# Fixed instruction orders, a shifted operand for frequency 256 and a mean row in one product in a fused spectral-filter and MLP kernel

## The chip, the cores and the metric

The kernel runs on one core of one Trainium2 chip. The metric is device time in microseconds (us). The kernel before takes 420.15 us, the median of three runs (419.25 to 421.0).

## The reference

One block of a network, forward and backward, in one launch. Sizes: S = 2048 rows, D = 512 channels, F = 1792 hidden units; everything is bf16 in memory.

```python
def _A_ref(x, w_r, w_i):                       # spectral filter
    X = jnp.fft.rfft2(x.astype(jnp.float32), axes=(-2, -1))
    X = X * (w_r + 1j * w_i)
    return jnp.fft.irfft2(X, s=(S, D), axes=(-2, -1)).astype(jnp.bfloat16)

def _B_ref(x, w1, b1, w2, b2):                 # MLP with squared ReLU
    h = jnp.einsum('bsd,df->bsf', x, w1) + b1
    r = jnp.where(h > 0, h, 0)
    return jnp.einsum('bsf,fd->bsd', r * r, w2) + b2

mod = (silu(c) @ w_mod).reshape(c.shape[0], 6, 1, -1)   # sa, ca, ga, sb, cb, gb
h = layernorm(x) * (1 + ca) + sa
x = x + ga * _A_ref(h, w_r, w_i)
h = layernorm(x) * (1 + cb) + sb
x = x + gb * _B_ref(h, w1, b1, w2, b2)
```

The outputs are this x and the gradients of its product with a given `grad_out` with respect to x, w_r, w_i, w1, b1, w2, b2, c and w_mod (ten arrays, `out_0` to `out_9`).

## The kernel before, in words

**Rows and tiles.** The 2048 rows are 16 tiles of 128 (`NT`), dealt so that partition p holds rows 16p to 16p+15; four tiles make one of the four blocks (`NB`) of the MLP. F is cut into 14 chunks of 128 (`NFC`).

**The transform as matrix products.** The Fourier transform over rows is split into two factors, the one over channels is made shorter by folding (sums and differences of mirrored quarters, on VectorE). The forward transform has the stages F1 (L286, L287: product `psA` with the table `TA`), F2 (L324: `psB` with `Cd`, emptied into `AE` by ScalarE in L329) and F3 (L310: `psC` with `LF`, emptied into `Xs` in L312), then a complex product with the weights on VectorE (`cmul`). The inverse goes G1 (`spec_g1`, L345: `psG` with `LG`, emptied into the array `CS`, which profile lines call `utcs`), G2 (L376: `psT` with `Cf`, emptied into `Tsb` in L379) and G3 (L387: `psY` with `TAT`). The backward pass runs the same stages on the gradient.

A row of 512 real channels has 257 frequencies, 0 to 256. G1 takes the even and the odd ones of the first 256 as two sets of 128 columns of the operand `Z`. Frequency 256 is a column of its own: for it G1 has small products of one output partition each (`psF`, L358), four of them side by side in column tiles of the array, and eight copies of one partition (L366 and L368) that put their results into `CS` after the last of them.

The shift `sa` of the first layer norm acts on frequency 0 only. It enters F2 as a row, `dcrow`, in four products with an operand of one partition (L326), each after one of the four products (L324) of its first half.

**Stages in time.** Start-up builds the tables on POOL, VectorE and ScalarE, loads x, and computes the modulation vectors (`mod_row`, L604). F1 of all 16 tiles follows. Beside it and up to the first G2/G3 run the back products (`back_products`, L714: grad_out times w2, 56 groups of four products of 512 columns, emptied into `gab` by ScalarE in L719 or VectorE in L717 by turns). Then F2/F3, G1, and the MLP by block: G2/G3 with the second layer norm, hidden products (`stage_h`, L886), the outputs and the row gradients (`stage_o`, `stage_gn`, L915). From the second block on, the normed rows are brought into transposed form by a store (L838) and a transposing DMA load (`h2T`, L842). Column sums over rows (biases and modulation gradients) are products with a vector of ones: `colsums` (L776) runs four of them, for one tile of rows, in the four column tiles of the array, and accumulates in the bank `acc`; `colsums1` (L1290) does the same into `acc1` near the end. After the last block come the backward F2/F3 with the gradients of w1 (L1144) between, backward G1, then G2/G3 with the gradients of w2 (L1232), and the end of the w_mod gradients.

**What sets the order.** When the program is built, a scheduler turns the source into one fixed order of instructions for each engine. It goes by priorities: the order in the source, moved by `tc.high_priority()`, by the class `Priority` (the back products carry `Priority(tc, LATE)`, behind everything else that is ready), and by `tc.issue_after(x)`, which holds an instruction back until x has been issued. Semaphores then enforce the data dependences. DMAs are issued by the queue of the engine that calls `dma_start`; here nearly all come from SP, the loads of the spectral weights (`load_w`) and some stores from POOL, three from ScalarE at the start (L560, L561, L569).

**Buffers.** Tile pools hand out rotating buffers; a PSUM pool `bufs=2` alternates between two banks, and a product waits until the bank's last reader is done.

## Time and profile before

| what | value |
|---|---|
| median of three runs | 420.15 us (419.25 to 421.0) |
| profiled execution, span from first to last instruction | 416.3 us |
| profiled execution's own time | the page gives its span only; the median of the runs is 3.85 us longer |
| matmuls | 2407 in the program (2387 recorded), TensorE busy 391.7 us (94%) |
| VectorE, ScalarE, POOL busy | 343.7, 277.1, 60.6 us (83, 67, 15%) |
| DMA | 101.11 MB, mean 243 GB/s |
| granted TensorE clock | 1.000 |

Busy time of TensorE counts every moment in which a matmul is in flight; matmuls overlap, so it isn't work at peak rate. In groups of instructions a line gives the source line, the engine, output and inputs with their tile shape and sizes, the number, the busy time, the mean duration in ns, and the idle time just ahead of the group with what ended it. The tile shape is the part of the array in use: `128*128` is all of it, `128*32` a column tile of 32, `128*1` a column tile with one output column in use.

### The profile page before, as it was taken

The numbers are of one execution on the slowest core, as the hardware profiler recorded it, in microseconds if no ns is written. First come the engines' busy times: TensorE is split into PE (matmuls) and PEld (weight loads), VectorE is DVE, ScalarE is ACT, GpSimd is POOL, SyncE is SP. The second block draws the span as 40 slices with busy tenths as digits, with TensorE's granted clock in tenths as the row PEclk, the third lists the DMA queues.
The fourth block names the chain that finished last, engine by engine and source line by source line (L and its number), as shares of the span: only waits on it lengthen the run. The fifth ranks groups of instructions, "written<-read, shape, count | busy, mean of one in ns | idle before, by whom it ended". The sixth has DMA issues, their size and how long they took to land. (4 is left out here: it accounts for less than half of the span.)

```text
span 416.3 us, 7175 instructions
## 1 busy us (share of the span) xinstructions
PE 391.7 (94%) x2387; PEld 197.6 (47%) x2407; DVE 343.7 (83%) x827; ACT 277.1 (67%) x495; POOL 60.6 (15%) x147
## 2 busy tenths in 40 slices
PE   2789999999899999999999999999999999999996
PEld 0345445664444444444444444445555665444444
DVE  6899868977988578988897998964999784877885
ACT  4568699868884079338924776545655567897785
POOL 7437950000000000000000000001314520000000
PEclk9999999999999999999999999999999999999999
DMA  8999899979199459949976997998999999999994
GB/s 240 232 261 298 237 213 313 323 239 240 40 331 324 126 161 276 248 128 204 288 227 194 201 291 278 291 213 245 287 280 283 350 265 227 223 269 223 239 266 143
DMA packets 143923, 101.11 MB, mean 243 GB/s; under 512 B 99049, under 2 KB 126830, under 8 KB 143630
## 3 DMA queue, kind: packets, MB, share of 16 engines
q1 hardware_dynamic: 140394, 92.96, 84.1%
q0 software_dynamic: 2784, 7.10, 5.6%
q10 hardware_dynamic: 708, 0.59, 0.5%
q8 instruction: 19, 0.31, 0.3%
q14 instruction: 18, 0.15, 0.1%
HBM read 35.44 MB, written 41.60 MB: 185 GB/s over the span
## 5 line engine op out<-in xcount | busy, mean ns | idle before, releaser
L714 PE MATMUL mm<-gT,w2T 128*128 128x512 bf16 x224 | 57.9, 382 | 4.5 <-ACT gab L719 4.2
L1144 PE MATMUL mm<-gab,h_sb 128*128 128x448 bf16 x256 | 50.9, 352 | 0.0
L1232 PE MATMUL mm<-g_sb,hn 128*128 128x512 bf16 (+1 forms) x250 | 49.6, 352 | 0.8 <-ACT gw L1234 0.4
L915 PE MATMUL og<-w1T,gab 128*128 128x512 bf16 x219 | 49.9, 379 | 0.3
L915 PE MATMUL og<-w,h 128*128 128x512 bf16 x216 | 49.1, 379 | 0.4
L886 PE MATMUL mm<-h2T,w 128*128 128x512 bf16 x164 | 40.2, 379 | 0.5 <-ACT r L888 0.3
L1232 PEld LDWEIGHTS <-hn 128*128 128x128 bf16 x256 | 24.4, 98 | 23.4 <-issue 2.0
L1144 PEld LDWEIGHTS <-h_sb 128*128 128x128 bf16 x256 | 24.6, 98 | 21.8 <-issue 0.8
L886 PEld LDWEIGHTS <-w 128*128 128x128 bf16 x224 | 21.3, 98 | 27.7 <-issue 4.9
L915 PEld LDWEIGHTS <-h 128*128 128x128 bf16 x224 | 21.7, 98 | 25.6 <-DVE h L890 0.6
L915 PEld LDWEIGHTS <-gab 128*128 128x128 bf16 x224 | 21.6, 98 | 25.5 <-DVE gab L894 1.0
L714 PEld LDWEIGHTS <-w2T 128*128 128x128 bf16 x224 | 21.2, 98 | 24.2 <-issue 7.9
L888 ACT ACTIVATE r<-mm,b1col 128x512 bf16<-128x512 f32 x41 | 27.4, 688 | 6.3 <-DVE gab L894 3.3
L294 POOL MEMSET AE<- 128x2 bf16 x4 | 0.3, 103 | 188.5 <-DMA gh_dram<-gab 188.5
L928 ACT CAST G<-og 128x512 bf16<-128x512 f32 x16 | 9.2, 580 | 22.2 <-PE og L915 22.2
L329 ACT ACTIVATE AE<-psB 128x1024 bf16<-128x1024 f32 x16 | 21.8, 1363 | 1.8 <-PE psB L324 0.9
L719 ACT CAST gab<-mm 128x512 bf16<-128x512 f32 x36 | 21.0, 593 | 2.6 <-PE mm L714 2.3
L890 DVE TENSOR_TENSOR h<-r 128x1024 bf16<-128x1024 bf16 x28 | 19.2, 686 | 2.6 <-ACT r L888 2.5
L1148 ACT CAST gw<-mm 128x448 bf16<-128x448 f32 x16 | 8.6, 537 | 18.4 <-PE mm L1144 18.4
L477 DVE SCALAR_TENSOR_TENSOR gm_junk<-wmc,onef,gmbc 128x512 bf16<-128x512 bf16 x24 | 18.0, 750 | 3.3 <-ACT gmbc L467 2.2
L894 DVE TENSOR_TENSOR gab<-r,gab 128x1024 bf16<-128x1024 bf16 x28 | 19.2, 684 | 0.0
L379 ACT ACTIVATE Tsb<-psT 128x512 bf16<-128x512 f32 x32 | 18.5, 603 | 0.6 <-ACT utcs L368 0.5
(292 smaller groups left out, 818.5 us busy)
## 6 DMA issues: line engine op xcount, KB each, us to landing
h_dram<-h SPq DMA_DIRECT2D x28, 256.0 KB, 3.2
gh_dram<-gab SPq DMA_DIRECT2D x28, 256.0 KB, 3.6
w<-in_B_w_dram SPq DMA_DIRECT2D x2, 1792.0 KB, 9.0
wmc<-in_w_mod_dram SPq DMA_DIRECT2D x12, 256.0 KB, 5.8
wz_dram<-Z SPq DMA_DIRECT2D x8, 258.0 KB, 3.8
xs_dram<-Xs SPq DMA_DIRECT2D x8, 258.0 KB, 4.0
Z<-wz_dram SPq DMA_DIRECT2D x8, 258.0 KB, 6.0
Xb<-xs_dram SPq DMA_DIRECT2D x8, 258.0 KB, 8.2
```

The lines of the kernel that those rows point to most:

```text
L329: nc.scalar.activation(dst, ps.rearrange("p r (s e f) -> p (r s) e f", s=2, e=2), AF.Copy, scale=EF_S)
L379: K["Tsb"] = nc.scalar.activation(Tsb, ps, AF.Copy, scale=EF_S).ins
L477: nc.vector.scalar_tensor_tensor(out=junk, in0=wmc[:, i, :], scalar=K["onef"], in1=gmbc, op0=ALU.mult, op1=ALU.mult, accum_out=self.gsc[:, ...
L714: nc.tensor.matmul(ps, lhsT=w2T[:, dc, fc * P:(fc + 1) * P], rhs=gT[b][:, :, dc, :], start=(dc == 0), stop=(dc == 3))
L719: nc.scalar.copy(out=gaT[b][:, fc, :], in_=ps)
L886: nc.tensor.matmul(ps, lhsT=w1[:, dc, (fc + i) * P:(fc + i + 1) * P], rhs=h2T[b][:, :, dc, :], start=(dc == 0), stop=(dc == 3))
L888: nc.scalar.activation(r[:, i, :], ps, AF.Relu, bias=b1col[:, fc + i:fc + i + 1])
L890: nc.vector.tensor_tensor(h2, r, r, op=ALU.mult)
L894: K["gh"] = nc.vector.tensor_tensor(gh, r, gh, op=ALU.mult).ins
L915: nc.tensor.matmul(ps, lhsT=lhs(fc), rhs=rhs[:, fc, :], start=(fc == 0), stop=(fc == NFC - 1))
L1144: nc.tensor.matmul(ps[:, 0:W4], lhsT=h2_sb[:, t, dc * P:(dc + 1) * P], rhs=ghn[t // 4][:, t % 4, fs], start=(t == 0), stop=(t == NT - 1))
L1232: nc.tensor.matmul(ps[:, 0:w], lhsT=hns[fc][:, t, :], rhs=g_sb[:, t, c:c + w], start=(t == 0), stop=(t == NT - 1))
```

## The change

**Order.** A dictionary `ORDER` in the source holds, for each of the five engines, a permutation of its instructions, numbered as the source emits them. `set_order`, called last, adds an edge between each instruction and the next in this list; the edge is an order only, without a semaphore. All `high_priority`, `issue_after` and `Priority` are gone from the source. `Slots` takes the place of the tile pools: as many buffers as before, but each has a fixed name, and successive tiles take them in turn.

**Frequency 256.** In G1 the even frequencies are now taken from two views of `Z`: for the first output (`y = 0`) frequencies 0, 2, ..., 254 and for the second (`y = 1`) 2, 4, ..., 256, since the second of 0 is zero and of 256 only the second is needed. This makes two pairs of products of 128 columns where one pair of 256 was; the odd frequencies keep their pair of 256. `psF`, its products and its copies are gone, and its bank lets `psG` have six buffers for four. `build_cf` adapts the table `Cf`: the second set's frequencies start at 2, and the factor of the end frequency is applied per set.

**Mean row.** `dcrow` is written with its quarters in the order of `psB`, and one product over all 512 columns starts the bank; the four products of `UT` add to it.

The orders themselves also differ: the column sums of `acc` and `acc1` come in longer groups (four tiles of rows at a time), the back products mostly in groups of four, with others between. The PE order has 84 changes of tile shape before and 40 after. At the start, ScalarE issues the load of the last part of `w_mod` (L569) after the sigmoid and the four activations of L593, and SP issues the loads of x tiles 8 to 15 ahead of the halves of the transposed w2.

```diff
+class Slots:
+    def __init__(self, tc, name, bufs, **kw):
+        self.pool = tc.alloc_tile_pool(name=name, bufs=1, **kw)
+        self.bufs, self.turn = bufs, {}
+
+    def tile(self, shape, dtype, name, bufs=None):
+        n = bufs or self.bufs
+        k = self.turn.get(name, 0)
+        self.turn[name] = k + 1
+        return self.pool.tile(shape, dtype, name=f"{name}_{k % n}s" if n > 1 else name)
...
 def build_cf(tc, K, cpool, g, dr):
-    nc.vector.tensor_scalar(efc[:, 0:1], K["pidf"], 0.0, None, op0=ALU.is_equal)
-    nc.vector.tensor_scalar(efc[:, 1:2], efc[:, 0:1], 256.0, None, op0=ALU.mult)
-    nc.vector.tensor_scalar(efc[:, 2:3], efc[:, 0:1], math.sqrt(0.5) - 1.0, 1.0, op0=ALU.mult, op1=ALU.add)
+    for i, end in enumerate((0.0, 127.0)):
+        nc.vector.tensor_scalar(efc[:, i:i + 1], K["pidf"], end, None, op0=ALU.is_equal)
+    nc.vector.tensor_scalar(efc[:, 0:2], efc[:, 0:2], math.sqrt(0.5) - 1.0, 1.0, op0=ALU.mult, op1=ALU.add)
     for i in range(4):
-        nc.vector.tensor_scalar(f4[:, i:i + 1], K["pidf"], 2.0, efc[:, 1:2] if i == 1 else float(i // 2), op0=ALU.mult, op1=ALU.add)
+        nc.vector.tensor_scalar(f4[:, i:i + 1], K["pidf"], 2.0, (0.0, 2.0, 1.0, 1.0)[i], op0=ALU.mult, op1=ALU.add)
...
-    nc.vector.tensor_scalar(Cf[:, 0:2, :], Cf[:, 0:2, :], efc[:, 2:3], None, op0=ALU.mult)
+    for i in range(2):
+        nc.vector.tensor_scalar(Cf[:, i, :], Cf[:, i, :], efc[:, i:i + 1], None, op0=ALU.mult)
...
 def spec_f23(tc, K, UT, AEs, dc, dest, elementwise, after=lambda gi: None):
...
+                if extra:
+                    nc.tensor.matmul(ps[:, hh, :], lhsT=dc[0], rhs=dc[1], start=True, stop=False)
                 for c in range(4):
-                    fs = slice(P * c, P * c + P)
                     co = (0, 3, 1, 2)[c]
-                    os = slice(P * co, P * co + P)
-                    nc.tensor.matmul(ps[:, hh, os], lhsT=UT[:, c, 2 * gi + hh, :, :], rhs=K["Cd"][:, fs], start=True, stop=not extra)
-                    if extra:
-                        nc.tensor.matmul(ps[:, hh, os], lhsT=dc[0], rhs=dc[1][:, fs], start=False, stop=True)
+                    nc.tensor.matmul(ps[:, hh, P * co:P * co + P], lhsT=UT[:, c, 2 * gi + hh, :, :], rhs=K["Cd"][:, P * c:P * c + P],
+                                     start=not extra, stop=(c == 3 if extra else True))
...
 def spec_g1(tc, K, Z, CS, after=None):
-    with tc.tile_pool(name="psG", bufs=4, space=PSUM) as psG_pool, tc.tile_pool(name="psF", bufs=1, space=PSUM) as psF_pool:
-        psF = psF_pool.tile([P, 4, P], FP32, name="psF")
+    with Slots(tc, name="psG", bufs=6, space=PSUM) as psG_pool:
...
-                for ch in range(2):
+                for y in range(2):
                     for ri in range(2):
-                        nc.tensor.matmul(ps[:, ch, :], lhsT=Z[gi][:, hh, ri, ch:256:2],
-                                         rhs=K["LG"][:, n, ri:ri + 2, :].rearrange("p y m -> p (y m)"), start=(ri == 0), stop=(ri == 1))
+                        nc.tensor.matmul(ps[:, 0, P * y:P * y + P], lhsT=Z[gi][:, hh, ri, 2 * y:256 + 2 * y:2],
+                                         rhs=K["LG"][:, n, ri + y, :], start=(ri == 0), stop=(ri == 1))
+                for ri in range(2):
+                    nc.tensor.matmul(ps[:, 1, :], lhsT=Z[gi][:, hh, ri, 1:256:2],
+                                     rhs=K["LG"][:, n, ri:ri + 2, :].rearrange("p y m -> p (y m)"), start=(ri == 0), stop=(ri == 1))
...
-            if gi % 2 == 1:
-                for ri in range(2):
-                    for n in range(2 * gi - 2, 2 * gi + 2):
-                        q = 32 * (n % 4)
-                        nc.tensor.matmul(psF[q:q + 1, n // 4, :], lhsT=Z[n // 2][:, n % 2, ri, 256:257], rhs=K["LG"][:, n, ri + 1, :],
-                                         start=(ri == 0), stop=(ri == 1), tile_position=(0, q))
...
-        for i in range(4):
-            dst = CS[0:1, :, 1, i:16:4, :].rearrange("p t m b -> p m t b")
-            src = psF[32 * i:32 * i + 1, :, :].rearrange("p m (t b) -> p m t b", b=8)
...
+ENGINES = {"PE": "PE", "ACT": "Activation", "DVE": "DVE", "POOL": "Pool", "SP": "SP"}
+ORDER = {
+    "PE": (
+        "1-9 18-19 14-15 20-21 10-13 16-17 26-29 22-23 0 24-25 122-137 30-31 138-141 34-35 142-149 36-37 32-33 150-157 38-39 "
...
+def set_order(tc):
+    mine = {}
+    for i in tc.nc.cur_bb.bb.instructions:
+        kind = type(i).__name__
+        if kind.startswith("Inst") and kind != "InstRegisterMove":
+            mine.setdefault(str(i.engine).split(".")[-1], []).append(i)
+    edge = mybir.DependencyInfo(mybir.DependencyClass.NoSync, mybir.DependencyReason.DATA)
+    for name, runs in ORDER.items():
+        todo = mine[ENGINES[name]]
+        seq = []
+        for r in runs.split():
+            a, _, z = r.partition("-")
+            seq += todo[int(a):int(z or a) + 1]
...
+        for before, after in zip(seq, seq[1:]):
+            tc.add_manual_dep(after, before.name, edge, reason="order")
...
     psd = psM.tile([1, D], FP32, name="mod_ps", bufs=1)
     for c, neg in enumerate(((), (1, 3), (1, 2), (2, 3))):
-        fs = slice(P * c, P * c + P)
+        fs, co = slice(P * c, P * c + P), (0, 3, 1, 2)[c]
...
-            nc.tensor.matmul(psd[:, fs], lhsT=sacol[:, i, k:k + 1], rhs=K["Cd"][:, fs], start=(i == 0), stop=(i == 3))
+            nc.tensor.matmul(psd[:, P * co:P * co + P], lhsT=sacol[:, i, k:k + 1], rhs=K["Cd"][:, fs], start=(i == 0), stop=(i == 3))
...
-                with tc.issue_after(K["scales"]):
-                    nc.gpsimd.dma_start(Z[gi][p0_:p0_ + n, :, i, 0:DF], rows_)
+                nc.gpsimd.dma_start(Z[gi][p0_:p0_ + n, :, i, 0:DF], rows_)
...
-        with Priority(tc, LATE):
-            for fc in range(NFC):
...
+    set_order(tc)
```

## The prediction

> **What bounds the kernel now.** I read the page from the top, then its costliest groups, the waits of TensorE, and stretches of time.
>
> ```profile
> span 416.3 us, 7175 instructions
> ...
> PE 391.7 (94%) x2387; PEld 197.6 (47%) x2407; DVE 343.7 (83%) x827; ACT 277.1 (67%) x495; POOL 60.6 (15%) x147
> ...
> PE   2789999999899999999999999999999999999996
> ...
> DMA  8999899979199459949976997998999999999994
> ```
>
> TensorE has matmuls in flight for 94% of the span and is never below 8 tenths outside the two ends. The busy time says little about how close it is to its peak, since matmuls overlap, so I took the distances between the starts of consecutive matmuls. Where nothing waits they repeat: 216 ns for 512 columns, 189 for 448, 109 for 256, 56 for 128, and a quad of column tiles costs one 216. Summed over the program this undisturbed stream is 370.3 us. The first matmul starts at 5.8 us, the last ends the stream at 412.9, the rest is a tail of 3.4. So 416.3 = 5.8 + 370.3 + 36.8 + 3.4, and the 36.8 us of excess is all that an order can win back from TensorE. Its parts: 12.2 us before 40 us of the span (half-rate TensorE, first loads); 84 changes of array shape; the rest waits.
>
> What a shape change costs is seen in this stretch of the timeline (start, duration, engine, line):
>
> ```profile
> 156.22 1.03 PE L886 MATMUL pst<-h2T,w 128*128 128x512 bf16 x4
> 157.18 0.39 PE L776 MATMUL acc<-gp,ones_q 128*32 128x512 bf16 x1
> 157.18 0.39 PE L776 MATMUL acc<-y,ones_q 128*32 128x512 bf16 x1
> 157.19 0.39 PE L776 MATMUL acc<-G,ones_q 128*32 128x512 bf16 x1
> 157.19 0.39 PE L776 MATMUL acc<-q,ones_q 128*32 128x512 bf16 x1
> 157.41 0.38 PE L776 MATMUL acc<-gp,ones_q 128*32 128x512 bf16 x1
> ...
> 157.73 0.82 PE L886 MATMUL mm<-h2T,w 128*128 128x512 bf16 x3
> ```
>
> Quad to quad is 0.23 us with no change of shape; from the last quad (157.41) to the next 128x128 matmul (157.73) it is 0.32. Over the 77 changes that can be isolated the median excess is 95 ns: 84 of them are 8.0 us.
>
> The waits of TensorE (what, for what, us in total, times, longest), and four stretches (us; PE, PEld, DVE, ACT, POOL busy; clock; DMA share; GB/s):
>
> ```profile
> PE mm L714 <- ACT gab L719: 4.2, 8, 1.0
> ...
> PE psB L324 <- ACT AE L329: 1.5, 6, 0.4
> ...
> PE psT L376 <- ACT utcs L368: 0.4, 1, 0.4
> ```
>
> ```profile
> 62.00:73.00 11.00, 10.06 (x82) 6.46 (x81) 8.56 (x16) 10.99 (x19) 0.00 (x0) 1.00 1.08 309
> ...
> 104.00:125.00 21.00, 19.41 (x108) 8.94 (x107) 19.39 (x47) 17.82 (x34) 0.00 (x0) 1.00 0.60 187
> ...
> 156.00:208.00 52.00, 51.66 (x271) 22.93 (x274) 47.01 (x98) 35.30 (x64) 0.00 (x0) 1.00 0.95 230
> ...
> 312.00:364.00 52.00, 51.42 (x358) 29.44 (x358) 40.71 (x85) 34.10 (x66) 14.04 (x24) 1.00 1.08 270
> ```
>
> From 62 to 73 us ScalarE, which empties psB, psC and the back products, is full and TensorE waits for it; from 104 to 125 VectorE and ScalarE are both near full. By the distances, with 95 ns taken off per change, TensorE loses 10.4 us to waits from 40 to 140 us (1.5, 3.4, 1.3, 3.2 and 1.0 in stretches of 20), and 6.5 us from 220 to 400. From 140 to 220 nothing is left to win but the shape changes.
>
> **What the Trainium skill says.** "TensorEngine Tiling (Array Packing)", Key Properties: a change of tiling mode "drains the TensorE"; it gives no price, and the trace gives 95 ns. "TensorE: Matmul & The Clock Gate", Back-to-back issue gap: N/2.4 + 2.5 ns for an isolated warm matmul; the trace agrees (216 at 512, 56 at 128), and disagrees with the 131 ns that the section names for a sustained stream. "Perfetto Trace Analysis", Tensor Engine Instruction: ScalarE and VectorE are strict FIFO. So an evacuation listed behind one that is not ready is late too, under the old order and the new alike; both orders are fixed when the program is built.
>
> **The change part by part.** I counted in the two programs' instruction orders.
>
> Frequency 256 by a shifted operand (build_cf, spec_g1): 64 matmuls of 128x1 tiles go; they run as 16 quads, about 55 ns each: -0.9 us. Their groups bring 16 shape changes, counted below. The main products become four of 128 columns and two of 256 in place of four of 256: the same columns in 64 more matmuls, at 2.5 ns each: +0.2. The 64 extra weight loads hide under the matmuls (PEld 47%). Eight one-partition copies at the end (six of 578 ns on ScalarE, L368, two of 682 on VectorE, L366) go; they stand between spec_g1 and the first spec_g2, whose wait is the third line above (0.4), with a smaller one of 0.2 in the forward pass: -0.5, one shape change excluded. psG gets six buffers for four, out of psF's bank: with L345 idle 0.1 us in all, worth 0. build_cf's one more VectorE op is off the path: VectorE has 3.5 us free from 52 to 62 us; uncovered it would be under 0.3.
>
> Mean row: five matmuls over 512 columns instead of eight alternating ones. It removes 3 small matmuls and 8 of the changes, adding 1 or 2; priced with the changes.
>
> Shape changes: 84 before; 40 after, by count: 16 of the 44 are psF's, some seven the mean row's, the others come from column sums (acc, acc1) gathered four rows at a time instead of about two. 44 x 0.095 = -4.2 us. They lie where TensorE is 98 to 99% busy, so I credit them whole. The gathered sums keep their operands (gp, q2, G, y) longer; the slots are as many as before, and where a row buffer comes free late its next writer waits on VectorE, 47.0 of 52 us busy from 156 to 208, which leaves some 5 us of cover.
>
> Slots: same numbers of buffers under fixed names; nothing issued, 0.
>
> The order on five queues is the part that no count settles. It can remove up to 10.4 + 6.5 us of waits and can add its own. For it: the back products, one evacuation of 593 ns per four matmuls, no longer run twelve and more in a row beside the forward transform and the first inverse one but mostly four at a time between other products, and L714's eight waits cost 4.2 (1.6 of them from 40 to 140 us); semaphore waits fall on TensorE from 595 to 500, on ScalarE from 603 to 520, which alone changes no price. Against it: in undisturbed stream time the distance from a psC product to the next use of its bank and from a Tsb evacuation's input to psY stays at 0.7 to 0.9 us, where some 1.1 is needed, and psB's shortest distance falls from 1.1 to 0.9. ScalarE's work from 62 to 73 us is not reduced. Bounds 0 and -13; I take half of the first (-5) and a quarter of the second (-1.5).
>
> Start-up: ScalarE now issues the load of w_mod's last half after the sigmoid and four activations, near 7.3 us instead of 1.7; the second group of products needs it. Before it landed at 9.9, about 8 us after issue among others; alone I reckon 5 to 6, so 12.5 to 13.5, some 3 late; the psA products behind that group start at 14.6 before, so 2 of it reach them. POOL interleaves the Z loads (0.6 us of issue each) with the row statistics, which then queue behind loads: +0.3, more if a load has to wait for room in its queue. SP moves x rows 8 to 15 ahead of the transposed w2 halves, 4 to 6 us earlier, and the spread back products save most of L714's other 2.6 us of waits: -1.7. Net +0.6, bounds -3 and +3.
>
> Sum against the profiled execution: 416.3 - 4.2 - 0.9 + 0.2 - 0.5 = 410.9; -5.0 - 1.5 + 0.6 gives a span of 405.0. The median of the runs is 3.85 over the span (420.15 against 416.3): **408.9 us**.
>
> **The rivals.** Structure only: the order trades waits for waits in the ScalarE-full stretches. Then 410.9 + 0.6 + 3.85 = 415.4 us. For it, the unchanged distances and ScalarE's 10.99 of 11 us; against it, the 4.2 us at L714 that sit beside a stretch with room.
>
> Transfers give it back: DMA share is 1.08 from 312 to 364 us and 1.00 to 400. If the late stages (12 or so of the 44 changes, half the psF part, half the 1.5) run at the transfers' pace, 2.3 us are lost: 411.2. Against it: TensorE waited there for a transfer just 0.2 us in L1232.
>
> Slower, by one mechanism: the transposed activations h2T arrive late. In blocks 1 and 2 the last pair goes evacuation, scale, norm, h2r, store (2.1 us), transpose (3.3) before L886 may start, and nothing stands behind it in the list. The trace has 7 us of spare in block 1 (landed 144.6, needed 151.9); in the new order I count 1.2 us of stream, 2.4 in block 2. With structure alone (415.4) and block 3 like block 2, arrivals later by L than reckoned stall 3L - 6 us in all: 422.25 is passed at L = 4.3, and at 4.7 the stalls are 8.1 us and the time 423.5. For it: a store took 3.2 to 3.6 us when the queue was full; against it, SP has no other transfer just ahead.
>
> The change not doing what it says would be shape changes that cost nothing: the order would still stand, 412.9.
>
> **How the numbers follow.** Order and structure 0.58 (408.9, own range 403 to 413), structure only 0.18 (415.4), transfers 0.09 (411.2), changes worth nothing 0.03 (412.9), slower 0.12 (423.5). Faster takes the first four, less 0.05 for structure-only cases with a start-up loss of 3 us, which end within half a per cent: 0.83, 0.05, 0.12. Half a per cent, 418.05 to 422.25, is about what this measurement can tell from no change. The range, 400 to 418, takes the order at two thirds of its bound with a start-up gain of 2 at one end, and structure alone with a start-up loss of 3 at the other.
>
> **What would show it.** No psF lines and no waits at L376 for L368; one dcrow matmul; quads of column sums in fours with 0.22 to 0.23 us between; the work that stands from 156 to 260 us in 1 to 2 us less. L714's wait for gab under 2 us. Wrong if psB, psC or psY waits exceed the present 2.0 us together, if L886 waits for h2T, or if the first psA starts after 16.5 us.

## The result, and the profile after

The changed kernel takes 420.95 us (median of 20 runs, 416.66 to 425.35) where the kernel before takes 420.08 beside it (20 runs, 418.61 to 421.79): a ratio of 1.0014, 95% interval 0.9995 to 1.0034. On another chip it was 1.0027 [0.9998, 1.0056]. Nothing was gained; 11.3 us had been forecast. Its runs also spread over 8.7 us, those of before over 3.2.

The page of the kernel after, its profiled execution (421.2 us, span 419.1), the same lines as shown of before and the granted clock:

```profile
span 419.1 us, 7038 instructions
...
PE 383.9 (92%) x2380; PEld 200.9 (48%) x2404; DVE 342.9 (82%) x826; ACT 275.1 (66%) x489; POOL 61.7 (15%) x147
...
PE   1589898999999999989999999999999939999896
...
PEclk9999999999999999999999999999999968999999
```

TensorE is busy 8 us less, as a smaller stream with fewer changes asks, and yet the span is 2.8 us longer. The reader should see the 3 in TensorE's row and, from the same slice on, the 6 and the 8 in the clock's: TensorE stands still for most of one slice and then runs at a lower clock. Before, the row never fell below 8 outside the ends. The two spans don't compare quite like the two medians. Runs that list both take 1.7 to 1.9 us more than their span for the kernel before and 2.1 to 2.3 for the changed one. So the profiled execution of before took some 418.1 us (an estimate), 2 us under its median, while that of after lies at its median: some 2 of the 2.8 us come from which execution was profiled.

The waits of TensorE after (what, for what, us in total, times, longest):

```profile
PE psT_0s L372 <- ACT Tsb_0s L374: 5.7, 1, 5.7
...
PE mod_ps L715 <- ACT modb L717: 4.0, 1, 4.0
PE mod_ps L715 <- DMA wm_0s<-in_w_mod_dram: 2.4, 1, 2.4
PE mm_1s L987 <- DMA h2T<-h_dram: 1.4, 1, 1.4
...
PE mm_1s L820 <- ACT gab_0s L824: 1.0, 1, 1.0
```

The back products' wait for `gab` (now L820) fell from 4.2 to 1.0 us, as forecast. On top stands a wait that did not exist. The timeline of TensorE around it (start, us, engine, line; in brackets the idle time before, and who ended it):

```profile
337.00 0.39 PE L372 MATMUL psT_1s<-Cf,utcs 128*128 128x128 bf16 x4
343.13 0.27 PE L372 MATMUL psT_0s<-Cf,utcs 128*128 128x128 bf16 x1 [5.74 <-ACT Tsb_0s L374]
...
345.32 1.70 PE L1241 MATMUL mm_0s<-gab_0s,h_sb 128*128 128x448 bf16 x4
346.81 1.70 PE L1241 MATMUL mm_0s<-gab_1s,h_sb 128*128 128x448 bf16 x4
```

The first G2 products of the backward inverse transform ran at 336.8 to 337.3; the evacuation of the first of them (`Tsb`, L374) started only at 342.48. And during and after the 5.7 us without work the granted clock was 0.50, from 339.0 to 349.2 us: four products of 448 columns take 1.49 us from start to start at 345 to 348 us, where the padded kernel below takes 0.76.

To see where the rest went I split each span as in the prediction: the undisturbed stream, 95 ns per change of shape, and what is left of the distances between matmul starts in stretches of the span; "waits" therefore also holds what a lower clock costs. "Padded" and "cut" are the runs e1_pad and e16_again explained below.

| us | before | forecast change | after | padded | cut |
|---|---|---|---|---|---|
| to the first matmul | 5.8 | 0 | 5.5 | 5.4 | 5.5 |
| undisturbed stream (forecast with the 0.5 us of the one-partition copies) | 370.3 | -1.2 | 369.2 | 369.2 | 369.2 |
| shape changes (84; then 40) | 8.0 | -4.2 | 3.8 | 3.8 | 3.8 |
| waits to 40 us | 12.0 | +0.6 | 12.0 | 11.9 | 12.0 |
| waits 40 to 140 | 10.4 | -5.0 | 6.3 | 5.8 | 5.6 |
| waits 140 to 300 | 3.5 | -1.5 (with the next two) | 3.3 | 4.4 | 3.8 |
| waits 300 to 360 | 0.9 | | 12.2 | 5.9 | 1.6 |
| waits from 360 | 2.1 | | 2.5 | 2.9 | 2.5 |
| last start to the end | 3.4 | 0 | 4.3 | 4.6 | 4.3 |
| span | 416.3 | -11.3 | 419.1 | 413.8 | 408.2 |

Up to 300 us the changed kernel does nearly what was counted. It loses 11.3 us more than before in the 60 us after that. The table makes the experiments' task plain: what happens from 300 to 360 us?

The same 60 us in both traces (window, us, busy us of PE, PEld, DVE, ACT and POOL, granted clock, DMA share, that is the mean busy share of the DMA engines, which the profile can put above 1, and GB/s), before:

```profile
300.00:360.00 60.00, 59.47 (x421) 34.78 (x421) 48.98 (x104) 38.47 (x71) 16.82 (x28) 1.00 1.04 275
```

and after:

```profile
300.00:360.00 60.00, 51.40 (x357) 30.84 (x358) 42.92 (x91) 30.97 (x57) 15.74 (x26) 0.91 0.94 246
```

Every engine does less, and the DMA queues move less too. That is waiting, not a fuller engine or fuller DMA queues.

### The profile page after: what moved, and what is told of

It is laid out like the page before. It is cut to its first block, busy times and chain, and to the rows that moved or that the text cites. A ratio compares the mean times of both kernels' runs of the same rounds, so it can differ in the third digit from the quotient of the medians.

```text
span 419.1 us, 7038 instructions
## 1 busy us (share of the span) xinstructions
PE 383.9 (92%) x2380; PEld 200.9 (48%) x2404; DVE 342.9 (82%) x826; ACT 275.1 (66%) x489; POOL 61.7 (15%) x147
## 2 busy tenths in 40 slices
DMA packets 143921, 101.09 MB, mean 241 GB/s; under 512 B 99049, under 2 KB 126830, under 8 KB 143630
## 5 line engine op out<-in xcount | busy, mean ns | idle before, releaser
L987 PEld LDWEIGHTS <-w 128*128 128x128 bf16 x224 | 21.2, 98 | 26.6 <-DMA h2T<-h_dram 1.7
L820 PEld LDWEIGHTS <-w2T 128*128 128x128 bf16 x224 | 21.2, 97 | 20.3 <-issue 2.5
L987 PE MATMUL mm_1s<-h2T,w 128*128 128x512 bf16 x80 | 20.5, 379 | 1.4 <-DMA h2T<-h_dram 1.4
L987 PE MATMUL mm_0s<-h2T,w 128*128 128x512 bf16 x84 | 21.5, 379 | 0.0
L1326 PE MATMUL mm_0s<-g_sb,hn_0s 128*128 128x512 bf16 x77 | 17.9, 379 | 0.2
L1326 PE MATMUL mm_1s<-g_sb,hn_1s 128*128 128x512 bf16 (+1 forms) x80 | 16.4, 358 | 0.9 <-DMA hn_1s<-h_dram 0.9
L372 PEld LDWEIGHTS <-utcs 128*128 128x128 bf16 x128 | 10.4, 100 | 10.7 <-issue 2.9
L987 PE MATMUL pst<-h2T,w 128*128 128x512 bf16 x60 | 15.4, 379 | 0.0
L820 PE MATMUL mm_1s<-gT_0s,w2T 128*128 128x512 bf16 x56 | 14.4, 378 | 1.0 <-ACT gab_0s L824 1.0
L820 PE MATMUL mm_0s<-gT_0s,w2T 128*128 128x512 bf16 x56 | 14.3, 378 | 0.5 <-DVE gT_0s L738 0.3
L820 PE MATMUL mm_0s<-gT_1s,w2T 128*128 128x512 bf16 x56 | 14.4, 379 | 0.1
L820 PE MATMUL mm_1s<-gT_1s,w2T 128*128 128x512 bf16 x56 | 14.4, 379 | 0.0
L332 PEld LDWEIGHTS <-utcs 128*128 128x128 bf16 x128 | 9.6, 97 | 5.0 <-issue 1.9
```

The costliest lines, as they stand in the source:

```text
L332: nc.tensor.matmul(ps[:, hh, P * co:P * co + P], lhsT=UT[:, c, 2 * gi + hh, :, :], rhs=K["Cd"][:, P * c:P * c + P], start=not extra, stop= ...
L372: nc.tensor.matmul(ps[:, P * i:P * i + P], lhsT=CS[:, t, i].rearrange("p a b -> p (a b)"), rhs=K["Cf"][:, i, :], start=True, stop=True)
L820: nc.tensor.matmul(ps, lhsT=w2T[:, dc, fc * P:(fc + 1) * P], rhs=gT[b][:, :, dc, :], start=(dc == 0), stop=(dc == 3))
L987: nc.tensor.matmul(ps, lhsT=w1[:, dc, (fc + i) * P:(fc + i + 1) * P], rhs=h2T[b][:, :, dc, :], start=(dc == 0), stop=(dc == 3))
L1326: nc.tensor.matmul(ps[:, 0:w], lhsT=hns[fc][:, t, :], rhs=g_sb[:, t, c:c + w], start=(t == 0), stop=(t == NT - 1))
```

## The experiments

### The stall: a pool that grew into its neighbour's memory

Before each tile is first written, the program waits for whatever used that memory. Pools are laid out one behind another, and a new pool waits where it overlaps an old one that has ended. In the kernel before, the pool of small rows for the gradient of w_mod holds two buffers of 1 KB per partition called `b4r` (`bufs=2`), of which only one is ever used. `Slots` allocates a buffer when it is first asked for, so the changed kernel holds one. Everything behind it moves by 1 KB: in the built programs the pool of the final stage now ends at byte 130,944 of the partition and overlaps the backward pass's elementwise pool, which starts at 130,112. The first write into the final stage's pool is the `Tsb` evacuation. Among the semaphores it waits for are now those of the stores of `gW` (the gradients of w_r and w_i) out of that elementwise pool, the last issued by GpSimd at 334.30 us. In the kernel before it waits for none of them. ScalarE's timeline before (first line) and after (second):

```profile
343.06 1.08 ACT L379 ACTIVATE Tsb<-psT 128x512 bf16<-128x512 f32 x2 [0.52 <-ACT utcs L368]
...
342.48 0.60 ACT L374 ACTIVATE Tsb_0s<-psT_0s 128x512 bf16<-128x512 f32 x1 [5.76 <-DMA g_sb<-in_grad_out_dram]
```

The releaser in the second line is inferred, and wrong: in the trace the last `gW` store landed at 341.76 us, and ScalarE was past that store's semaphore at 341.82. It then went through its other waits, and the evacuation began. Two runs undo and repeat the overlap, and nothing else:

```diff
 # e1_pad: the changed kernel, plus one unused buffer
     endp["gw"] = gwp
+    gwp.pool.tile([P, D], BF16, name="b4r_1s")

 # e2_overlap: the kernel before, less its unused buffer
-            row = pool.tile([1, w], BF16, name="b4r", bufs=2)
+            row = pool.tile([1, w], BF16, name="b4r", bufs=1)
```

> The changed kernel with one unused tile of 1 KB per partition added to the pool gwp, so that gwp is as large as before the change and the pool fin2 under it no longer reaches 832 bytes into the region of the pool ewb. Nothing else differs, the order included. Theory A (the first write into fin2, the evacuation of psT into Tsb, waits for the last stores of the gW tiles only because the two pools touch; that idles TensorE 5.7 us and then leaves it at half rate for some 3 us): no wait of psT for Tsb over 0.5 us, no dip of the granted clock near 340 us, time 411 to 413. Rival B (the order of the tables itself is at fault: three groups of psT in a row on TensorE with no other product between, or transfers that are late anyway): the wait moves to another line in the same place and the time stays at 418 to 421.

> The kernel before with one edit: the tile b4r gets one buffer in place of two, of which only one was ever used. That shrinks gwp by the same 1 KB and lets fin2 touch ewb. Theory A: the first Tsb evacuation of the backward pass now waits for the gW stores here too. The last of them is issued at 335.4 us and stores of this kind took 5.9 to 9.0 us to land, so up to 344.4, against a first psT at 342.6: a stall of 0 to 2 us, time 420 to 422.5. Rival B: no wait of Tsb for a store, and 420 as before.

e1_pad took 417.29 us, ratio 0.9893 [0.9871, 0.9914]; repeated on another chip, e1_again gave 416.33, ratio 0.9910 [0.9884, 0.9937]. e2_overlap took 423.96, ratio 1.0076 [1.0046, 1.0106]. The stall went and came as theory A said, but both times missed: e1_pad is over 4 us slower than its 411 to 413, and e2_overlap above its 422.5. The evacuation on ScalarE's timeline, in the padded kernel,

```profile
339.76 0.60 ACT L374 ACTIVATE Tsb_0s<-psT_0s 128x512 bf16<-128x512 f32 x1 [0.54 <-PE psT_0s L372]
```

and in the kernel before without its unused buffer:

```profile
348.07 1.08 ACT L379 ACTIVATE Tsb<-psT 128x512 bf16<-128x512 f32 x2 [3.80 <-DMA out_dram<-gW]
```

The one waits 0.54 us for its product, the other 3.80 us for the store of `gW`, by name: the last of these landed at 347.92 us. 1 KB that nothing uses is worth 1.2% to the changed kernel (5 us, between ratios of different chips) and 0.8% to the kernel before. On a third chip the changed kernel itself was run again:

> The changed kernel as it is, beside the padded variants on one chip. Theory A (the first backward Tsb evacuation waits for the gW stores of the pool that lies under its own): ratio to before 0.998 to 1.004 as in its first runs, TensorE idle some 5 to 6 us at the first psT product after 335 us. Rival B (the 420.95 was its chip's doing): ratio near the padded kernel's 0.989 to 0.991.

424.8 us, ratio 1.0027, the one given at the start; TensorE stood for 3.8 us at the same place. So the stall isn't one chip's doing.

> The changed kernel with the unused 1-KB slot back in pool gwp, once more, as the base for the three edits that go with it. Every theory: a ratio to the kernel before of 0.989 to 0.995, as in its first run (0.9893). Its waits for transfers in 40 to 100 and 300 to 340 us of the span should come again, about 1 to 3 us and 6 us; if these vary by more than 2 us between the two chips, the order's gain depends on how fast small stores land.

It came within its forecast ratio. Its losses moved: 3.3 us from 80 to 100 us where the first run lost 1.4, and 4.3 from 300 to 360 where that lost 5.9. By its two ratios the padded kernel gains 4.5 and 3.8 us, not 11. What holds back the rest?

### Structure alone

e3_struct gives the kernel before only the shifted frequency and the single mean row, with its own scheduler for the order (64 changes of shape):

```diff
-                    if extra:
-                        nc.tensor.matmul(ps[:, hh, os], lhsT=dc[0], rhs=dc[1][:, fs], start=False, stop=True)
+                if extra:
+                    nc.tensor.matmul(ps[:, hh, :], lhsT=dc[0], rhs=dc[1], start=True, stop=False)
...
-                for ch in range(2):
+                for y in range(2):
-                        nc.tensor.matmul(ps[:, ch, :], lhsT=Z[gi][:, hh, ri, ch:256:2],
-                                          rhs=K["LG"][:, n, ri:ri + 2, :]...)
+                        nc.tensor.matmul(ps[:, 0, P * y:P * y + P], lhsT=Z[gi][:, hh, ri, 2 * y:256 + 2 * y:2],
+                                         rhs=K["LG"][:, n, ri + y, :], ...)
```

> The kernel before with the two changes of the products alone: frequency 256 by the shifted operand (with six psG buffers) and the mean row in one product. The order stays with the scheduler. By the prediction's terms: 16 shape changes of psF and some 7 of the mean row at 95 ns are 2.2 us, psF's quads 0.9, the small copies 0.5, less 0.2: 3.4 us faster, 416 to 417.5. A rival in which these lie beside other waits: no difference, 419.5 to 420.5.

424.21 us, ratio 1.0044 [1.0009, 1.0078]: missed by 7 us. The waits of TensorE and ScalarE's timeline say where:

```profile
PE psY L376 <- ACT Tsb L368: 4.9, 2, 4.6
```

```profile
95.07 0.60 ACT L368 ACTIVATE Tsb<-psT 128x512 bf16<-128x512 f32 x1 [4.91 <-DMA xs_dram<-Xs]
```

The same kind of wait in the forward pass: the first `Tsb` there also writes where a pool has just ended, and that pool's last `Xs` store took 9.9 us to land behind the load of w1 (1.8 MB). In the kernel before, the same store took 9.6 us and landed at 92.70; its first `Tsb`, behind the one-partition copies that e3 no longer has, started at 93.11, and ScalarE had no idle time there. e7 holds that load back in e3, e8 does it in the kernel before:

```diff
-        nc.sync.dma_start(w1, w1_view)
+        with tc.issue_after(K["x1"]):
+            nc.sync.dma_start(w1, w1_view)
```

> The two changes of the products alone, as in the third run, with the load of w1 (1.8 MB) issued behind that of the first x1 rows and no longer ahead of the last xs store. In the third run TensorE stood 4.6 us at psY: the first Tsb of the forward pass waited for that store, which took 9.9 us to land behind the w1 load. Theory: the store lands in about 4 us, the wait goes, and the 3.4 us of the products become visible against the next run: 415.5 to 417.5 where that one is at 419 to 421. Rival: the products give nothing and this run equals the next one.

> The kernel before with the moved w1 load alone, the control for the run above. Its forward Tsb waited little (TensorE's excess from 80 to 100 us was 1.3 us without the shape changes), so at most 1 us is to be had: 419 to 421. If w1 comes late for the first hidden products, it is slower than before by what they wait.

e7 took 420.85, ratio 0.9956 [0.9919, 0.9992]; e8, the control, 423.66, ratio 1.0013 [0.9973, 1.0053]. In e7 the wait is gone. Structure is worth 2.8 us between the two medians. Each ratio is known to some 1.6 us, so the difference to some 2.3: it is above nothing, not much more. The two profiled executions lie the other way round (spans 421.7 for e7, 419.9 for e8), and e7's lost 2.8 us from 340 to 360 us where e8's lost 1.0. The expectation had 3.4; with the 20 changes that the program really loses, not 23, its terms give 3.1: 0.7 of stream, 1.9 and 0.5 for the copies. In e3 a store that is late at a pool's turn took all of it.

### The order's own waits for stores, 300 to 360 us

In the padded kernel VectorE (first fence) and TensorE (second) lose time at 310 to 318 us:

```profile
314.68 0.43 DVE L418 TENSOR_TENSOR gW_1s<-p_1s 128x514 bf16<-128x514 bf16 x1 [4.04 <-issue]
...
316.24 0.75 DVE L472 SCALAR_TENSOR_TENSOR gm_junk<-wmc_1s,onef,gmbc 128x512 bf16<-128x512 bf16 x1
```

```profile
317.72 0.92 PE L1241 MATMUL mm_0s<-gab_0s,h_sb 128*128 128x448 bf16 x4 [2.43 <-ACT gmbc L462]
```

The buffer `gW_1s` is free for its next content when its four stores have landed. SP's table strews these from 296.4 to 308.2 us among five loads and five stores of other buffers. The first landed 6.4 us after its issue; for the last the trace has no landing, but VectorE goes on 6.5 us after its issue, at 314.68. The profile names no releaser ("issue"), so that VectorE waits for this store is inferred here, from the times. VectorE stands for 4.0 us, `gm_junk` behind it is late, ScalarE's `gmbc` waits for `gm_junk`'s buffer, and TensorE waits for `gmbc`. The prediction had priced such chains, one queue behind another, only for h2T. e5_stores groups the stores, e10_cd moves another late store (that of the table Cd, which the forward `Tsb` waits for), e11_mid does both and puts the LGb load ahead:

```diff
 # SP's table, e5_stores
-209 227 ... 217 221 208 207 219 216 215 ... 214 210 229 ... 224 218 233
+209 208 207 210 227 ... 217 219 216 218 221 215 ... 214 229 ... 224 233
 # e10_cd
-27 21 ... 42 26 48
+27 26 21 ... 42 48
 # e11_mid: both of these, and
-213 225 ... 223 230 228
+213 230 225 ... 223 228
```

> The padded kernel of the first run with SP's order changed in one place: the four stores of the second gW tile, which its table strews from 296.4 to 308.2 us between loads, are issued one after the other as in the kernel before, and so are the four of the third. Theory A: VectorE's stop of 4.0 us at 310.7 (its next write into the same gW buffer waits for the last of these stores) goes, and with it the waits that it passes on: ScalarE's copy into gmbc behind VectorE's gm_junk (4.0), TensorE's 2.4 us at L1241 behind that. TensorE's excess between 300 and 340 us falls from 6.0 to about 2, the time by 3 to 4 us under the first run, to 413 to 414.5. Rival B: transfers are short there, another of them is late next, and the time is that of the first run within 1 us.

> The padded kernel with the store of Cd moved on SP's queue to just behind the first LF_dram store. Theory A (the first forward Tsb evacuation writes into the region of the pool that has just ended, and waits for that pool's last store, which the tables made the Cd store): 80 to 100 us loses 1 to 3 us less to waits, time 0.8 to 3 us below the padded kernel's. Rival B (the last xs store lands as late as the Cd store did, and takes its place): less than 0.5 us.

> As the run with the Cd store moved, and on SP's queue the gW stores of the second column half grouped by their buffer, with the LGb load put ahead of them, behind the Z6 load. Theory A (6 us of TensorE waits in 300 to 340 us come from where the tables put these stores and this load among one another): 300 to 340 us loses about 2 us instead of 6, time 3 to 5 us below the run with Cd alone. Rival B (the transfers together are late, whatever their order: DMA queues are full there): another wait for a transfer comes in its place, and the gain is under 1 us.

e5 took 420.52, ratio 0.9940 [0.9909, 0.9971]: no gain on the padded kernel, where 3 to 4 us were expected. VectorE's stop of 4.0 us was gone, one of 1.7 us for another `gW` buffer stood near the same place, and TensorE had a new wait:

```profile
PE psG_5s L352 <- DMA LGb<-LG_dram: 3.4, 1, 3.4
```

e10 took 417.97, ratio 0.9932 [0.9905, 0.9958], beside 0.9910 for the padded kernel: its stretch from 80 to 100 us lost 1.3 us where the padded kernel lost 3.3 on that chip, and 320 to 340 lost 4.7 where it lost 1.5. e11 took 416.4, ratio 0.9914 [0.9890, 0.9937]; 300 to 360 lost 5.0. Neither of the two gained on the padded kernel. So each late store can be put in time, and something else is then late. By these runs alone one could not say whether the order or the transfers as a whole are at fault. Hence the cut: both kernels with the `gW` stores shortened to 8 rows of partitions each. So cut, the kernels leave out most of the gradients of w_r and w_i; they show only where the time goes.

```diff
-                        K["gW"] = nc.sync.dma_start(rows_, gW[p0_:p0_ + n, i, :, 0:DF]).ins
+                        K["gW"] = nc.sync.dma_start(rows_[0:8], gW[p0_:p0_ + 8, i, :, 0:DF]).ins
...
-                        nc.gpsimd.dma_start(rows_, gW[p0_:p0_ + n, i, :, 0:DF])
+                        nc.gpsimd.dma_start(rows_[0:8], gW[p0_:p0_ + 8, i, :, 0:DF])
```

> The padded kernel with each store of the two spectral weight gradients cut to 8 of its 32 or 64 rows of partitions: most rows of those two outputs are left out, nothing else. Theory A (the waits in 300 to 360 us are for these stores, and for transfers that stand behind them): 300 to 360 us loses about 1 us instead of 4 to 6, DMA share there falls by a third or more, time 3 to 5 us below the padded kernel's. Rival B (these waits come from the order of VectorE, ScalarE and TensorE among themselves): 300 to 360 us loses 4 us or more as before, gain under 1 us.

> The padded kernel with the same cut, beside it. Theory A: ratio to before 0.972 to 0.982, so that against the cut kernel before the new order and structure are worth 8 to 11 us, near what the prediction counted. Rival B: within 5 us of the cut kernel before.

> The kernel before with each store of the two spectral weight gradients cut to 8 rows of partitions: most rows of those two outputs are left out, nothing else. Theory A (only the new order stands behind these stores; before loses 1 us in all from 300 to 360 us): 0 to 1.5 us faster than before, ratio 0.996 to 1.0. Rival B (these stores bound both kernels): 4 us or more, ratio 0.990 or less.

The padded kernel so cut took 411.51 us, ratio 0.9726 [0.9663, 0.9789], and on another chip 411.88, ratio 0.9781 [0.9744, 0.9818]. Beside the latter the kernel before, so cut, took 419.11, ratio 0.9947 [0.9920, 0.9974]. Bytes moved fell only from 101.09 to 99.27 MB, and packets by 1,904 of 143,921. VectorE at the place of the 4.04 us, in e16_again:

```profile
309.25 0.43 DVE L418 TENSOR_TENSOR gW_1s<-p_1s 128x514 bf16<-128x514 bf16 x1 [0.34 <-DVE p_1s L416]
```

and TensorE's 60 us (columns as above), in the padded kernel and in e16_again:

```profile
300.00:360.00 60.00, 55.41 (x397) 33.14 (x395) 47.78 (x104) 37.06 (x68) 15.72 (x26) 1.00 0.95 255
...
300.00:360.00 60.00, 58.81 (x428) 35.28 (x429) 49.76 (x108) 40.60 (x77) 15.19 (x26) 1.00 0.93 241
```

TensorE is at 58.81 of 60 us there, with DMA share 0.93; the padded kernel has 55.41 at 0.95. The share had been expected to fall by a third. So it doesn't tell whether stores are late, and the waits of this stretch were for the `gW` stores, or for what stood behind them. Whether their bytes or their place in the order makes them late isn't separated: the cut changes both, and it does not make a store land at once. Cut from 64.2 to 8.0 KB, those that GpSimd issues still took 4.7 to 6.4 us to land (medians of the three buffers), the full ones 6.5 to 7.0. The cut is worth some 5 to 8 us to the padded kernel (0.9910 against 0.9781 and 0.9726, different chips), and 2.2 us to the kernel before. Its span in the trace stayed at 416.3 us because both profiled executions are fast ones (418.12 is the lowest of the eight runs), so no trace shows where the 2.2 us are. Rival B, 4 us or more for both kernels, falls, and theory A holds in kind; the kernel before's ratio is a little below its forecast of 0.996.

With these stores out of the way the new order and structure are worth 7.2 us on one chip (411.88 against 419.11; known to some 2 us), under the 8 to 11 of the expectation, but not 0.

### The start-up order

The changed kernel's first `psA` products start at 16.1 us (14.6 before). Five runs put parts of the start-up orders back, in the padded kernel. ScalarE's table in e4b and the later ones, as an example, with 4 the load of w_mod's second half, 10 the evacuation of the second modulation row and 0 the table TA:

```diff
 # ACT: e4b_evac
-2-3 5-9 4 0 14 10 1 11
+2-10 0 14 1 11
 # ACT: e6_start, e12_start, e14_start3, e15_best
-2-3 5-9 4 0 14 10 1 11
+2-9 0 10 14 1 11
 # POOL: e6, e12 (row scales of tiles 0 to 3 ahead of the Z loads); e14, e15 (of tiles 0 to 7)
-7-8 34 12 38-39 35 40 46 41 36 73 18 37 79 20 31 42 88 27 47 ...
+7-8 12 34-41 46 73 18 79 20 31 42 88 27 47 ...
+7-8 12 34-49 73 18 79 20 31 88 27 ...
```

e6, e12 and e14 also take VectorE's row statistics and folds ahead of its table work; e12 brings the `ones` and the scaling of gT forward too, e14 the first `gab` evacuation ahead of a row normalisation. e15_best is e14 with e11's edits.

> The padded kernel of the first run with two entries of ScalarE's order moved at the start: the load of w_mod's last part goes ahead of the sigmoid again, and the evacuation of the first modulation row goes ahead of the activation that builds TA, which waits for VectorE until 11.0 us. If the start-up costs what the trace shows (the second group of products waits 4.0 us for that evacuation, and the first psA starts at 16.1 us against 14.6 before), the second group starts near 10.9 and the first psA near 14.5, and the time falls by 1 to 2 us under the first run. If psA waits for x and its fold anyway, the two runs are equal within 0.4 us.

> The padded kernel with the start-up of three queues put back into an order like that before: on VectorE the angles of TA ahead of the row statistics and the first two rows' statistics, norm and fold ahead of the later rows', on POOL the first pair's rstd chain ahead of the second's, on ScalarE the early w_mod load, and the first modulation row ahead of the first scaled row. If the start-up of the tables is at fault for what the trace shows (TA at 11.0 us against 7.5, first psA at 16.1 against 14.6), the first psA starts at 14.0 to 14.8 and the time falls by about 1.5 us under the first run. If what follows waits for w2T and gT anyway, the gain is under 0.5.

> The padded kernel with the start-up orders of ScalarE, VectorE and GpSimd put back near those of the kernel before (w_mod's second half loaded early, row statistics ahead of the Z loads on GpSimd, ones and gate scalings early). Theory A (the first psA products at 16.1 instead of 14.6 us come from these orders): first psA at 14 to 15 us, time 1 to 1.5 us below the padded kernel's. Rival B (the start is set by the transfers of w_mod and x, not by the orders): first psA at 16 us as before, no gain.

> As the padded kernel with the old start-up orders, and further: the evacuation of the first back product on VectorE ahead of the row normalisation that it was queued behind, and on GpSimd the row scales of rows 4 to 7 ahead of the Z loads. Theory A (the start-up orders of the tables cost 1 to 3 us): the first psA at 13 to 14 us, no wait of 6 us for gab, the first 40 us lose 8 to 9 us instead of 11.5 to 12, time 2 to 3 us below the padded kernel's. Rival B (what the start gains is lost again at the next evacuation or transfer): first psA early, but the first 40 us lose 11 us or more, no gain.

> The edits joined: padded slot, Cd store earlier, grouped gW stores with LGb ahead of them, and the start-up orders of the last run. If the parts add up as measured singly (padded 0.990, Cd and stores 0 to -1 us, start -2 to -3 us): ratio 0.981 to 0.986. If waits for transfers move on as they did singly: 0.988 to 0.992, as the padded kernel.

Measured: e4b 419.13, ratio 0.9927 [0.9898, 0.9956]; e6 423.82, 0.9998 [0.9958, 1.0038] (the mean row's column product waited 3.7 us for its operand of ones, a `memset` that I had left late); e12 422.9, 1.0064 [1.0041, 1.0087]; e14 421.39, 0.9944 [0.9916, 0.9972]; e15 422.09, 0.9988 [0.9959, 1.0018]. None beats the padded kernel. e12 shows why an order that is early in one place is late in another. VectorE's and TensorE's timelines:

```profile
19.57 0.18 DVE L750 BATCH_NORM_AGGREGATE l_mv_1s<-l_st_2s 128x2 f32<-128x6 f32 x1
22.78 0.58 DVE L761 TENSOR_SCALAR x_sb<-x_sb,inv,l_nb_3s 128x512 bf16<-128x512 bf16 x1 [3.04 <-POOL l_nb_3s L755]
...
24.48 0.67 DVE L825 CAST gab_0s<-mm_0s 128x512 bf16<-128x512 f32 x1
```

```profile
25.20 1.86 PE L823 MATMUL mm_0s<-gT_0s,w2T 128*128 128x512 bf16 x4 [5.91 <-DVE gab_0s L825]
```

The last product that fills this buffer was through at 18.4 us; its evacuation stood behind a normalisation that waited for GpSimd. e14 mends this, and the first `psA` came at 13.15 us, 3 us earlier than in the padded kernel. Then TensorE's timeline in e14 goes on:

```profile
23.99 0.28 PE L294 MATMUL psA_0s<-TA,fold_u_0s 128*128 128x256 bf16 x1 [2.28 <-DVE fold_u_0s L258]
...
29.83 0.58 PE L823 MATMUL mm_1s<-gT_0s,w2T 128*128 128x512 bf16 x1 [2.20 <-ACT gab_0s L827]
```

It lost 15.0 us in the first 40 us against 11.9 in the padded kernel: rival B of e14's expectation, the 3 us gained were given back twice over, here by the next rows' folds and the next evacuation. After the second of these stops the granted clock was 0.50 for 3.4 us. So the start of the tables was no loss that these five runs could mend: 12.0 us of waits in 40 us before and after.

## Why the prediction was wrong, point by point

**Structure: right.** The stream fell by 1.1 us (0.7 had been counted) and the changes from 84 to 40 as counted; the median price per change was 96 ns in the traces after (95 before). Alone, with no store in the way, structure measured 2.8 us, known to some 2.3, where its terms give 3.1 (e7 against e8).

**Waits from 40 to 140 us: right.** Counted -5.0, found -4.1 in the changed kernel and -4.6 in the padded one. L714's wait (now L820) fell to 1.0.

**Start-up: about right in size, by luck in part.** The forecast was +0.6, the waits to 40 us are the same. The first `psA` at 16.1 stayed short of the 16.5 that was named as a sign of error, though the second half of w_mod was not what held it: the waits show 4.0 us for the evacuation of `modb`, which stands in ScalarE's list behind TA. "Perfetto Trace Analysis", Tensor Engine Instruction, has ScalarE and VectorE strict FIFO, each working off its list in order; e12's 5.91 us agree.

**"Slots: same numbers of buffers under fixed names; nothing issued, 0": the step that failed.** The number of buffers was not the same (the description of the change has it wrong too), by one that nobody used, and where a buffer lies decides what its first write waits for. It cost 1.2% of the time, some 5 us, the half-speed stretch included. Nothing was issued; yet a wait was added that no diff shows, only the addresses and the semaphores of the built programs.

**"A quarter of the second (-1.5)": the other step that failed.** From 140 us the padded kernel waits 6.7 us more than before, not 1.5 less: 0.9 from 140 to 300, 5.0 from 300 to 360, 0.8 after. With the `gW` stores cut it is 1.4 more. The bound, 0 to -13, let the order only win; the chance that fixed orders put stores where buffers are awaited stood in a rival, "transfers give it back" at 2.3 us, that reasoned from the queues' share. The share was 0.94 to 0.95 in the slow stretch, 0.93 in the cut one and 1.04 in the kernel before, which waits least: it does not tell. The end of the span (last start to the end) took 0.9 to 1.2 more, which was not in the sum. Together: of the 14.1 us between the forecast span (405.0) and the one found (419.1), 13.0 are waits from 140 us on.

**The rivals.** The slower one named a late transfer behind which nothing else stands; h2T did wait, 1.4 us after, far from its 8.1. The kind was right, a store or load that the fixed order made late, but at another place: `gW`, not h2T. "Structure only" fits the padded kernel's time by chance: 416 to 417 us against 415.4, though the waits before 140 us did go. "Changes worth nothing" is excluded: the changes cost 95 to 96 ns each. Its time should read 413.1 by the prediction's own terms (408.9 and 4.2), not 412.9.

**The signs.** Two of the three signs of being wrong appeared: in the changed kernel the waits of psB, psC and psY were 2.4 us together where 2.0 was the mark, and L886's products (now L987) waited 1.4 us for h2T. Neither is where the time went.

**The range**, 400 to 418, holds the padded kernel's medians and not the changed one's. It ended there because both failed steps were allowed no loss at all. Its lower end leaves out the 3.85 us from the span to the median: two thirds of 13 and a start-up gain of 2 give 404.

## What to carry to other kernels

A change of buffers costs nothing only if addresses, too, are compared: where one pool begins in the memory of another that has just ended, its first write waits for that pool's last stores, and a kilobyte decided here. In a fixed order, ask for each store which buffer it frees and who writes there next; a store can land late without the DMA share showing it. Putting that one store in time was not enough in e5, e10 and e11. Moving an instruction forward pays only if the next one on the path can follow it.

## What the runs showed of the hardware

Half speed after a stop: after 5.7 us without work 448 columns took 373 ns (1.49 us for four) until about 349 us. Once the first 20 us are over, every stop of TensorE of 3 us or more in the kept traces was followed by a granted clock of 0.50, for 3.4, 6.8 or 10.2 us (3.0 us in e2_overlap, 3.4 in e5, 3.8 in after_again, 4.6 in e3, 5.7 in after). Of the shorter stops some were and some were not. The same wait in after_again (first two lines, followed by 3.4 us at 0.50) and in the padded kernel (last two, at full clock):

```profile
319.52 1.65 PE L1241 MATMUL mm_0s<-gab_0s,h_sb 128*128 128x448 bf16 x4 [2.34 <-ACT gmbc L462]
320.97 1.70 PE L1241 MATMUL mm_0s<-gab_1s,h_sb 128*128 128x448 bf16 x4
...
317.72 0.92 PE L1241 MATMUL mm_0s<-gab_0s,h_sb 128*128 128x448 bf16 x4 [2.43 <-ACT gmbc L462]
318.47 0.92 PE L1241 MATMUL mm_0s<-gab_1s,h_sb 128*128 128x448 bf16 x4
```

"TensorE: Matmul & The Clock Gate", What's actually happening, has the clock fall to half after an idle window of some 3.4 us. The lengths of these stretches agree with a window of 3.4 us; but stops of 2.0 (e12), 2.1 (e10), 2.2 (e14) and 2.3 us (after_again) were enough here, so a stop need not last 3.4 us. This is a likely part of the changed kernel's spread, an estimate: a stretch of 3.4 us at half clock takes 0.004 off the mean clock of 420 us and up to 1.7 us of TensorE's work, and that mean lay between 0.986 and 0.996 in its 20 runs.

Small stores landed late: a store of `gW_1s`, 64.2 KB, needed 6.4 us from issue on SP to landing in the padded kernel, and an `Xs` store 9.9 us behind 1.8 MB. The last eight `gW` stores that GpSimd issued in the changed kernel, from 326.6 to 334.3 us, took 7.5 to 10.0 us. "DMA: Bandwidth & Descriptors", Anatomy of one DMA, gives about 2.0 us of fixed time for a DMA issued by GpSimd, most of it the wait for the write's receipt; none of these stores came near it, while a store of `h2r` in the kernel before, issued on SP at 139.2 us, took 2.1.

What stays open: which of the remaining waits in the cut kernel (1.4 us more than before after 140 us) belong to h2T and the final stage, where the kernel before's 2.2 us went when its stores were cut, and whether an order exists that keeps the 7.2 us with whole stores. The fastest version that writes all of its outputs is the padded kernel, 0.9893 [0.9871, 0.9914] and 0.9910 [0.9884, 0.9937] of the time before.
